# One PSUM tile for u and z of the 64-row jobs

**Chip, cores, metric.** One core of one Trainium2 chip. The metric is the time of one execution on the device in microseconds, lower is better; runs that are compared come from the same rounds on the same chip. In this program the engine PE does the matmuls, ACT and DVE work on their results, and SP issues the transfers of the output. PSUM holds the tiles that matmuls write, SBUF the others.

## The reference, cut to what matters

The program is forgetting attention followed by a spectral mix and a ReLU. Only its end matters here:

```python
u = x + y                                    # x: attention, y: filtered in 64 Fourier modes
return u + np.maximum(u @ w_ch, 0.0)         # 8 batches x 576 rows x 512, float32, 9.44 MB
```

With z = u @ w_ch, the kernel has x and x @ w_ch (`XW`) in SBUF already; in its last 32 us it adds the last modes of y to both, in PSUM, and writes u + max(z, 0).

## The kernel before

The 576 rows of a batch are four blocks of 128 and one of 64. The output stage runs 20 jobs: jobs 0-3, 5-8, 10-13 and 15-18 take two blocks, jobs 4, 9, 14 and 19 ("singles") the 64-row blocks of two batches. A PSUM tile `[128, 2, 512]` float32 is two banks of 512 columns; u has two tiles, z has two. A pair uses both banks of a tile, a single only the first.

```python
psPair = [{"u": psE, "z": psE}, {"u": psU}]          # later: psPair[1]["z"] = psX
def start(n, tags="uz"):
    return [psPair[n % 2][tag].tile([128, 2, D], F32, tag=tag, name="p" + tag) for tag in tags]
...
def emit_u(job, ps, u, split=False):                 # ACT takes u out of PSUM
    ...  nc.scalar.copy(u[:, bs, :], ps[0][:, bs, :])
def emit_o(job, ps, u, o, pair, split=False):        # DVE: max(z, 0) + u, then SP sends
    ...  nc.vector.scalar_tensor_tensor(o[:, bs, :], ps[1][:, bs, :], 0.0, u[:, bs, :], ALU.max, ALU.add)
    ...                                              # singles: 2 transfers from 64 partitions each
    ...                                              # pairs from job 7 on: rows of two jobs go together,
    ...                                              # 2 transfers of 512 KB from 128 partitions
for n, job in enumerate(jobs):                       # z of this job, u of the next one
    zs = terms(job, ps, 1, "xy" if n else "y")
    us = []
    if not last:
        nxt = start(n + 1)
        us = terms(jobs[n + 1], nxt, 0, "xy")
    ...
    elif wide(job):        run(zs); run(us)
    elif len(job) == 1:    run(us); run(zs)
    ...
    emit_u(jobs[n + 1], nxt, uo_n[0])
    emit_o(job, ps, *uo, n == 0)
```

(Cuts are marked by dots; two `run` calls are drawn on one line.) A tile is given to its next user when the last reader of the one before has finished with it.

The softmax here doesn't subtract the row's maximum and nothing guards it: scores larger than these inputs give would overflow.

## Time and profile before

| | before |
|---|---|
| median of the first 3 runs | 436.66 us (436.33 to 436.97) |
| PE, DVE, ACT busy | 368.1, 263.7, 224.4 us of 435.2 |
| bytes written | 9.44 MB, all in the last 32 us |
| DVE's last pass ends, SP's last issue ends | 427.1 us, 430.7 us |

Busy shares over the whole span say nothing about this change, because it lives in the last 7% of it. The view to read is the timeline of the output stage: who waits for whom around jobs 9, 14 and 19, and how full the DMA engines are meanwhile. The prediction shows those lines.

### The profile page before, as it was taken

How to read it: one execution, taken by the hardware profiler on the slowest of the kernel's cores; microseconds unless marked ns; L12 is line 12 of the kernel's file. 1: busy time of each engine (PE TensorE's matmuls, PEld its weight loads, DVE VectorE, ACT ScalarE, POOL GpSimd, SP SyncE). 2: the span in 40 equal slices, each digit the busy share in tenths (PEclk: the TensorE clock that was granted, in tenths of full speed). 3: DMA queues.
4: the chain of work that ended last, by engine and by line, in shares of the span. 5: the costliest groups of instructions: out<-in, count | busy, mean ns of one | idle time of the engine just before them, and what ended most of it. 6: DMA issues, size and time to landing. Idle time of an engine off the chain costs nothing.

```text
span 435.2 us, 12314 instructions
## 1 busy us (share of the span) xinstructions
PE 368.1 (85%) x5313; PEld 249.7 (57%) x5313; DVE 263.7 (61%) x659; ACT 224.4 (52%) x339; POOL 126.8 (29%) x198
## 2 busy tenths in 40 slices
PE   3787799999987879778787788799999998899881
PEld 2454566776666666566565666656665555454540
DVE  5797888876555655555557568533332665553892
ACT  2887488774526454365462646134434443631781
POOL 8333332333233233232333222223223223200400
PEclk9996899996558665586565869589999999989997
DMA  8999999999999999999999999999999999995797
GB/s 184 234 235 241 234 236 238 235 212 236 234 215 236 225 224 237 210 238 233 214 237 211 212 211 212 211 211 211 211 211 211 212 210 211 211 211 100 253 367 274
DMA packets 50982, 97.38 MB, mean 224 GB/s; under 512 B 3792, under 2 KB 12976, under 8 KB 50928
## 3 DMA queue, kind: packets, MB, share of 16 engines
q0 software_dynamic: 46560, 86.09, 100.9%
q1 hardware_dynamic: 4368, 10.51, 6.7%
q8 instruction: 41, 0.67, 0.6%
q14 instruction: 13, 0.11, 0.1%
HBM read 163.73 MB, written 9.44 MB: 398 GB/s over the span
## 4 chain that ended last, share of the span: by engine, by line
PE 35%; DMA 26%; ACT 12%; DVE 10%; issue 4%; SPq 0%; DVEq 0%; POOL 0%; ACTq 0%
DMA wb<-in_moe_w_i_dram 25%; ACT E L576 8%; PE pav L614 7%; PE ps L569 7%; PE A L188 6%; PE tp L307 5%; PE px L657 2%; PE vp L541 2%; DVE QTs L322 2%; ACT KT L320 2%; ACT VT L326 2%; DVE XT L671 1%; DVE os L1005 1%; DVE E L591 1%; PE px L682 1%
## 5 line engine op out<-in xcount | busy, mean ns | idle before, releaser
L576 ACT ACTIVATE E<-ps 128x1024 bf16<-128x1024 f32 (+1 forms) x128 | 101.5, 851 | 26.1 <-PE ps L569 15.4
L93 POOL DMA_DIRECT2D wb<-in_moe_w_r_dram x64 | 42.5, 664 | 128.9 <-PE A L188 25.1
L188 PE MATMUL A<-XT,wb 128*128 128x16 bf16 x1984 | 69.9, 181 | 8.2 <-DMA wb<-in_moe_w_i_dram 3.8
L188 PEld LDWEIGHTS <-wb 128*128 128x128 bf16 x1984 | 63.5, 100 | 22.8 <-issue 11.9
L569 PE MATMUL ps<-QTs,KT 64*128 64x64 bf16 (+4 forms) x384 | 60.2, 334 | 16.6 <-ACT E L576 14.7
L93 POOL DMA_DIRECT2D wb<-in_moe_w_i_dram x64 | 42.3, 661 | 77.5 <-DMA wb<-in_moe_w_i_dram 32.5
L614 PE MATMUL pav<-va,E 128*128 128x65 bf16 (+1 forms) x1088 | 57.1, 214 | 3.2 <-DVE x_all L636 2.6
L614 PEld LDWEIGHTS <-E 128*128 128x128 bf16 (+1 forms) x1088 | 47.0, 118 | 16.9 <-issue 7.0
L591 DVE TENSOR_TENSOR E<-E,trimask 128x256 bf16<-128x256 bf16 (+2 forms) x128 | 36.9, 303 | 20.0 <-ACT E L576 19.8
L326 ACT COPY VT<-tp 128x640 bf16<-128x640 bf16 (+1 forms) x32 | 23.2, 761 | 33.4 <-PE tp L307 33.4
L867 ACT CAST XW<-pxw 128x512 bf16<-128x512 f32 x36 | 20.7, 586 | 35.9 <-PE pxw L860 28.3
L569 PEld LDWEIGHTS <-KT 64*128 64x128 bf16 x384 | 19.4, 100 | 33.6 <-issue 22.8
L860 PE MATMUL pxw<-wch,yy 128*128 128x512 bf16 x144 | 36.0, 388 | 0.0
L320 ACT COPY KT<-tp 128x640 bf16<-128x640 bf16 (+1 forms) x32 | 21.9, 749 | 26.0 <-PE tp L307 25.8
L910 ACT CAST XW<-pB 128x512 bf16<-128x512 f32 x36 | 21.0, 585 | 25.4 <-PE pB L828 25.3
L909 DVE CAST x_all<-pA 128x512 bf16<-128x512 f32 x36 | 24.9, 692 | 14.2 <-PE pA L828 12.5
L322 DVE COPY QTs<-tp 128x640 bf16<-128x640 bf16 (+1 forms) x32 | 23.4, 767 | 14.3 <-PE tp L307 14.0
L636 DVE TENSOR_TENSOR x_all<-pav,rcp 128x384 bf16<-128x384 f32 x64 | 29.1, 455 | 0.9
L625 DVE RECIPROCAL rcp<-pav 128x6 f32<-128x6 f32 x64 | 12.1, 189 | 25.1 <-PE pav L614 24.3
L828 PEld LDWEIGHTS <-ident_bf 64*64 64x64 bf16 (+1 forms) x348 | 15.7, 108 | 17.9 <-issue 9.3
L153 DVE TENSOR_TENSOR YTe<-A,Yacc 128x128 bf16<-128x128 f32 x16 | 5.9, 367 | 33.3 <-PE A L188 33.3
L541 PE MATMUL vp<-ident_bf,VT 128*128 128x128 bf16 x160 | 18.4, 261 | 4.6 <-DVE QTs L322 3.9
(142 smaller groups left out, 617.4 us busy)
## 6 DMA issues: line engine op xcount, KB each, us to landing
wb<-in_moe_w_r_dram POOLq DMA_DIRECT2D x62, 512.0 KB, 16.7
wb<-in_moe_w_i_dram POOLq DMA_DIRECT2D x62, 512.0 KB, 17.3
stv<-in_v_dram POOLq DMA_DIRECT2D x10, 576.0 KB, 15.2
out_dram<-os SPq DMA_DIRECT2D x10, 512.0 KB, 4.5
stk<-in_k_dram POOLq DMA_DIRECT2D x11, 288.0 KB, 15.3
stq<-in_q_dram POOLq DMA_DIRECT2D x11, 288.0 KB, 15.1
wx<-in_v_dram POOLq DMA_DIRECT2D x5, 576.0 KB, 15.4
out_dram<-uo SPq DMA_DIRECT2D x3, 512.0 KB, 3.6
```

Source lines behind the costliest of these rows:

```text
L93: keep(nc.gpsimd.dma_start(dst, src))
L188: ins = nc.tensor.matmul(A[:, eb, mi, :], lhsT=w_of(mi, eb * 128), rhs=x_of(m), start=(i == 0), stop=(i == len(terms) - 1),)
L320: nc.scalar.copy(rows(KTs[pr % 2][:, :, 0:S]), tv)
L322: ins = nc.vector.tensor_copy(rows(QT[pr][:, :, :]), tv)
L326: nc.scalar.copy(rows(VTs[pr % 2][:, :, 0:S]), tv)
L541: nc.tensor.transpose(vp[:, sc, :, :].rearrange("p b d -> p (b d)"), VTs[s // 2 % 2][:, h, sc * 128 : (sc + 1) * 128], ident_bf[:, :],)
L569: nc.tensor.matmul(ps[:, b, o : o + n], lhsT=KTs[pr % 2][bs, h, jb * 128 : (jb + 1) * 128], rhs=QT[pr][bs, h, jb * 128 + c0 : jb * 128 + c ...
L576: nc.scalar.activation(E[:, :, piece * 512 : piece * 512 + w], ps[:, :, 0:w], ACT.Exp, scale=scale,)
L591: nc.vector.tensor_tensor(dg, dg, tr, ALU.mult)
L614: nc.tensor.matmul(pav[64 * half : 64 * half + w, slot, :], lhsT=E[:, b, c : c + (w - 1) * st + 1 : st], rhs=va[:, jb, b, :], start=(n == ...
L636: nc.vector.tensor_tensor(xo, pi, ri, ALU.mult)
L860: nc.tensor.matmul(pxw[:, :], lhsT=xT[:, eb, i * 128 : (i + 1) * 128], rhs=wch[:, eb, :], start=(eb == 0), stop=(eb == NDC - 1),)
```

## The change

Its intent: a single needs only one bank for u and one for z. If both lie in the single's u tile, the z tiles are left to the pairs, and z of the pair behind a single finds a tile that has been free for a while.

```diff
-        def start(n, tags="uz"):
-            return [
-                psPair[n % 2][tag].tile([128, 2, D], F32, tag=tag, name="p" + tag)
-                for tag in tags
-            ]
+        def bank(tag, n):
+            return psPair[n % 2][tag].tile([128, 2, D], F32, tag=tag, name="p" + tag)
+
+        def start(n):
+            u = bank("u", n)
+            if len(jobs[n]) == 1:
+                return [u[:, 0:1, :], u[:, 1:2, :]]
+            return [u, bank("z", sum(len(j) == 2 for j in jobs[:n]))]
```

## The prediction

> **What bounds the kernel now.** I read first the page, then the list of waits from 408 us on, then the timeline of the last 28 us engine by engine, and last the busy time and DMA rate in half-microsecond stretches. The change touches only the output stage, so what bounds the first 400 us (the weight transfers, 25% of the chain that ended last) is out of it.
>
> The output stage has 20 jobs. Jobs 0 to 3, 5 to 8, 10 to 13 and 15 to 18 are pairs of row blocks (PSUM tiles of two banks), jobs 4, 9, 14 and 19 are the 64-row singles. Each job is: PE writes u and z into PSUM, ACT copies u out (L1000), DVE forms max(z,0)+u from PSUM and the copy (L1005), SP sends the rows out. I told the jobs apart in the timeline by counting: the 692 ns forms of L1005 on 128x512 at 415.09, 420.76 and 426.46 are jobs 9, 14 and 19.
>
> The waits from 408 us on (waiting group, what ended it, us in total, times, longest):
> ```profile
> ACT us L1000 <- PE pu L828: 3.2, 5, 1.0
> PE pz L828 <- DVE os L1005: 1.8, 5, 0.5
> DVE os L1005 <- issue: 0.7, 2, 0.5
> PE pz L828 <- DVE uo L1005: 0.7, 1, 0.7
> ```
> PE waits 2.5 us in six places for DVE to free z's banks. Those behind singles are what the change aims at. Around job 9:
> ```profile
> 414.61 0.38 PE L828 MATMUL pz<-yy,BIl 64*64 64x512 bf16 x2
> 415.19 0.37 PE L828 MATMUL pz<-x_all,ident_bf 64*64 64x512 bf16 x1 [0.20 <-DVE os L1005]
> 415.62 0.38 PE L828 MATMUL pu<-x_all,ident_bf 64*64 64x512 bf16 x1
> 415.09 0.69 DVE L1005 SCALAR_TENSOR_TENSOR uo<-pz,uo 128x512 f32<-128x512 f32 x1
> 415.93 1.23 DVE L1005 SCALAR_TENSOR_TENSOR os<-pz,us 128x1024 f32<-128x1024 f32 x1
> 416.31 1.01 ACT L1000 COPY us<-pu 128x1024 f32<-128x1024 f32 x1 [0.69 <-PE pu L828]
> 417.36 1.23 DVE L1005 SCALAR_TENSOR_TENSOR os<-pz,us 128x1024 f32<-128x1024 f32 x1 [0.20 <-ACT us L1000]
> ```
> z of job 9 is through at 415.0. z of job 10 starts at 415.19, when job 8's DVE pass (413.92 + 1.23 = 415.15) has left the bank. u of job 11 follows on PE at 415.62, ACT copies it at 416.31, and only then (417.36) can DVE take job 11. So the DVE gap ahead of job 11 is set by u of job 11, not by z.
>
> But does DVE set the end? The stretches (length, busy time of PE, PEld, DVE, ACT, POOL, then granted clock, DMA share, GB/s):
> ```profile
> 416.00:418.00 2.00, 1.91 (x39) 1.07 (x29) 1.79 (x2) 1.69 (x2) 0.00 (x0) 1.00 1.02 395
> 418.50:419.00 0.50, 0.37 (x8) 0.25 (x9) 0.50 (x2) 0.50 (x1) 0.00 (x0) 1.00 0.92 279
> 419.00:419.50 0.50, 0.50 (x14) 0.30 (x8) 0.50 (x1) 0.33 (x1) 0.00 (x0) 1.00 0.54 143
> 419.50:420.00 0.50, 0.50 (x12) 0.43 (x8) 0.50 (x2) 0.27 (x1) 0.00 (x0) 1.00 0.98 209
> 420.50:424.00 3.50, 2.98 (x48) 1.64 (x48) 3.11 (x4) 2.66 (x3) 0.00 (x0) 1.00 1.03 411
> 426.00:431.00 5.00, 0.08 (x2) 0.00 (x0) 1.14 (x2) 0.02 (x1) 0.00 (x0) 0.78 1.02 408
> ```
> DVE is done at 427.1 while the DMA engines carry 408 GB/s until 431. SP shows why:
> ```profile
> 416.08 2.60 SPq L1012 DMA_DIRECT2D out_dram<-uo  x2
> 418.76 3.30 SPq L1025 DMA_DIRECT2D out_dram<-os  x4
> 422.16 2.69 SPq L1012 DMA_DIRECT2D out_dram<-uo  x2
> 424.94 3.22 SPq L1025 DMA_DIRECT2D out_dram<-os  x4
> 428.25 2.49 SPq L1012 DMA_DIRECT2D out_dram<-uo  x2
> ```
> From 418.76 SP issues without a break worth naming; job 19's rows, ready at 427.1, are issued at 428.25. From there the end is a sum of bytes: four pairs of 2 x 512 KB and two singles of 2 x 128 KB are 4.72 MB; at 408 GB/s that is 11.6 us, and with about 1 us from issue to full rate it gives 431.4, as seen. The last moment at which the DMA engines ran dry is 418.5 to 420.0 (about 0.7 us lost, worked out from 279, 143 and 209 against 408 GB/s). So the end hangs on when rows 10 and 11 go out: job 11's DVE pass ends at 417.36 + 1.23 = 418.59, while SP is free of job 9's issues at 416.08 + 2.60 = 418.68.
>
> **What the Trainium skill says.** "PSUM — Partial Sum Buffer", section "Engine vs sequencer instructions": matmuls start and complete in program order. The trace agrees: u of job 11 (415.62) stands behind z of job 10 (415.19), so a wait moved from z to the u behind it still stops PE. "Perfetto Trace Analysis", section "Matmuls": independent groups should rotate through banks so that emptying one overlaps filling the next; the trace shows the lack of it as the 0.2 to 0.7 us waits of pz, which is the change's intent. The same page, section "What 'DMA-bound' means": a solid row of DMA instructions on the issuer points to the issuer as the bound, that window being descriptor generation. Here SP is solid, yet the engines carry 408 GB/s at share 1.02, so I take the solid row as back-pressure, not as the bound. "DMA: Bandwidth & Descriptors", section "Where 436 GB/s comes from", gives 435 GB/s for the ports and about 358 for one core's HBM share; the trace's 408 lies above the second, so near the first there is little left.
>
> **The change, part by part.** No instruction is added or removed: the same matmuls, copies, DVE passes and transfers. Only tiles move.
>
> Part 1, z of a pair. It alternated by job number, so z of job n waited for DVE of job n-2. Now it alternates by the count of pairs. After a single, z of job n waits for n-3: z of 5 for job 2 (not 3), z of 10 for 7 (not 8), z of 15 for 12 (not 13). One job later, 6, 11 and 16 wait for the pair ahead and no longer for the single. Worth: z of job 10 starts right behind z of job 9, about 414.6 to 414.8 instead of 415.19; DVE's job 10 can follow job 9's pass at about 415.75 instead of 415.93 (passes follow a 692 ns one after 0.6 us): 0.18 us earlier. z of job 5, waiting now until 409.39, starts near 408.5; DVE's job 5 moves from 410.48 to about 409.9, 0.6 us earlier.
>
> Part 2, the single's u tile. It now holds z as well, so it is freed by the single's DVE pass and no longer by ACT's short copy. The next user is u two jobs on: u of 6 waits for DVE's job 4, u of 11 for job 9, u of 16 for job 14. Job 9's pass ends at 415.09 + 0.69 = 415.78. With job 8's pass perhaps 0.07 later, u of job 11 can start at about 415.89, against 415.62 now: 0.27 us later. ACT's copy goes from 416.31 to 416.58, DVE's job 11 from 417.36 to 417.63, its end from 418.59 to 418.86. What part 1 gave job 10 is not passed on, as job 11 was held by u and is held longer. For job 6 the same: job 4's pass ends at 409.94, u of 6 goes from 409.82 to 409.98, DVE's job 6 from 411.62 to about 411.72, so the 0.6 us of job 5 shrink to -0.1 within one job. For job 16: job 14's pass ends near 421.44 + 0.27, u moves from 421.32 to about 421.75, DVE's job 16 from 423.06 to about 423.5.
>
> Part 3, the path that sets the end. SP sends rows 10 and 11 after job 11: now 418.76, then about 418.86 + 0.09 = 418.95, so 0.19 us later, with the engines dry meanwhile. Everything behind follows at the DMA rate. Job 16 would end at 424.7 against an issue at 424.94 (+0.19), job 19 at 427.6 against 428.25: both hidden. Earlier gains (jobs 5 and 10) land ahead of the dry spell and vanish in it. Sum: +0.19 us, 436.66 + 0.19 = 436.85.
>
> **The rivals.** One: u does not wait for the single's pass as I read it (because the release is kept by bank, say), and the intent holds. Then z of 10 and u of 11 move up by about 0.4 us, DVE's job 11 starts at 416.9, and rows 10 and 11 are ready at 418.1. SP still has to finish job 9's issues at 418.68, itself held by back-pressure, so the direct gain is under 0.1 us; with some of the dry spell filled it could reach 0.7 us at most: 436.0 to 436.6. For it speaks that the DMA has a hole of just that size; against it SP's 416.08 + 2.60. Two: DVE is the bound, at 1.79 of 2.00 us busy from 416 to 418. Then the moved wait on u costs 0.27 to 0.43 us per single, and three singles give up to 1.0 us: 437.6. Against it: job 19's rows wait 1.1 us for SP, so the tail hides most. Three: the end is bytes alone and all shifts are hidden: 436.66. Four: the order of instructions on PE comes out different because the tiles differ; that could go either way by some tenths.
>
> **Range and chances.** The whole stage lasts 32 us, its floor is 9.44 MB written at 408 GB/s, 23 us; no step above is worth over 1 us, and 2% would be 8.7 us. Three runs of the kernel before spread 0.64 us. So the range is rival one's floor to rival two's ceiling, nearly: 436.1 to 437.5. Faster or slower by 2% would need something unseen; 0.01 each.
>
> **What would show it.** Right: L1005 of job 10 moves up beside job 9; pu of job 11 waits for DVE uo where it waited for none; ACT's copy ahead of job 11 starts near 416.6; the DMA hole at 419 is as deep or longer; SP's issue of rows 10 and 11 near 418.95. Wrong: pu of job 11 starts near 415.2 and DVE's job 11 before 417.3, or the hole at 419 fills. The prediction fails altogether if the instructions of the first 400 us are placed differently, which nothing in the change asks for.

## The result, and the profile after

The changed kernel took 437.13 us (median of 6, 436.39 to 438.34), the kernel before 436.82 us (median of 6, 436.33 to 437.03). The ratio is 1.0013, with a 95% interval of 0.9997 to 1.0029. A ratio is the mean time of one kernel's fast runs over that of the other's of the same rounds, so not quite the ratio of the medians quoted.

The profiled run after happened to be a short one (434.7 us against 435.2), so spans do not tell the two apart. Positions inside the stage do. I count them from the first DVE pass of job 0 (403.99 before, 403.85 after), and write +13.37 for 13.37 us after it. PE's order of matmuls is the same in both kernels until the output stage (the first that differs is number 5,102 of 5,313, at +4.1), and there it differs only around the singles.

Who waited for whom from 404 us on, after:

```profile
DVE os L1008 <- ACT us L1003: 1.9, 3, 0.6
PE pz L828 <- DVE os L1008: 1.9, 3, 0.6
PE pu L828 <- DVE uo L1008: 1.5, 3, 0.7
PE pu L828 <- ACT uo L1003: 1.2, 3, 0.7
```

The two last rows are new. The first of these is the wait that the prediction moved from z to u; the second, PE held by ACT's copy of a single's u, it did not name. "PE pz <- DVE uo", 0.7 us before, has gone: the intent is met. Around job 9, PE, then DVE, then ACT:

```profile
414.58 0.40 PE L828 MATMUL pu<-XW,ident_bf 64*64 64x512 bf16 x2 [0.25 <-ACT uo L1003]
415.01 0.37 PE L828 MATMUL pz<-x_all,ident_bf 64*64 64x512 bf16 x1
416.04 0.37 PE L828 MATMUL pu<-x_all,ident_bf 64*64 64x512 bf16 x1 [0.41 <-DVE uo L1008]
415.29 0.69 DVE L1008 SCALAR_TENSOR_TENSOR uo<-pu,uo 128x512 f32<-128x512 f32 x1 [0.24 <-issue]
415.90 1.21 DVE L1008 SCALAR_TENSOR_TENSOR os<-pz,us 128x1024 f32<-128x1024 f32 x1
417.75 3.49 DVE L1008 SCALAR_TENSOR_TENSOR os<-pz,us 128x1024 f32<-128x1024 f32 x3 [0.64 <-ACT us L1003]
416.71 2.84 ACT L1003 COPY us<-pu 128x1024 f32<-128x1024 f32 x3 [1.27 <-PE pu L828]
```

The matmuls at 414.58 are z of job 9; they carry the name pu because they write the u tile now. They wait 0.25 us for ACT's copy of u out of the other bank. DVE's job 9 (415.29) therefore has a gap of 0.24 us ahead of it. z of job 10 starts at once (414.6 to 415.01). u of job 11 (416.04) waits for DVE's job 9 to end, ACT's copy follows, and DVE's job 11 (417.75, at +13.90 against +13.37) has a gap of 0.64 us where it had 0.20. SP after:

```profile
416.01 2.10 SPq L1015 DMA_DIRECT2D out_dram<-uo  x2
419.00 3.09 SPq L1028 DMA_DIRECT2D out_dram<-os  x4
422.20 2.31 SPq L1015 DMA_DIRECT2D out_dram<-uo  x2
425.19 3.17 SPq L1028 DMA_DIRECT2D out_dram<-os  x4
428.46 2.47 SPq L1015 DMA_DIRECT2D out_dram<-uo  x2
```

SP is no longer solid: it is free at 418.11 and issues rows 10 and 11 at 419.00, free at 424.51 and issues rows 15 and 16 at 425.19. It now waits for DVE. But its issues take less time each, and the DMA rate is what it was:

```profile
418.50:420.00 1.50, 0.97 (x18) 0.72 (x20) 1.50 (x2) 1.05 (x2) 0.00 (x0) 1.00 0.70 213
426.00:431.00 5.00, 0.89 (x8) 0.14 (x3) 2.12 (x3) 0.58 (x1) 0.00 (x0) 1.00 1.00 399
```

(Same columns as in the prediction; the DMA share is the mean busy share of the 16 DMA engines.) I call the stretch of low rate behind a single a hole. The hole behind job 9 moves 213 GB/s against 210 in the same 1.5 us before (the mean of the prediction's three stretches), and the tail 399 against 408. DVE ends 1.4 us later, SP's last issue begins 0.27 us later (+25.75 against +25.48), and the data cease (the last packet of output begins) at +28.6 after and +29.0 before, where the last 0.7 us is a trickle under 125 GB/s. These ends scatter by some tenths from profile to profile, so a shift of 0.2 us is not to be seen in them.

### The profile page after: what moved, and what is told of

The parts are those of the page before. It is cut to its first block, busy times and chain, and to the rows that moved or that the text cites. A ratio compares the mean times of both kernels' runs of the same rounds, so it can differ in the third digit from the quotient of the medians.

```text
span 434.7 us, 12314 instructions
## 1 busy us (share of the span) xinstructions
PE 363.7 (84%) x5313; PEld 246.8 (57%) x5313; DVE 263.0 (61%) x659; ACT 223.6 (51%) x339; POOL 126.9 (29%) x198
## 4 chain that ended last, share of the span: by engine, by line
DMA 43%; PE 23%; ACT 10%; DVE 7%; issue 4%; POOL 1%; ACTq 0%
DMA wb<-in_moe_w_i_dram 39%; ACT E L576 6%; PE pav L614 5%; PE ps L569 5%; PE A L188 4%; PE tp L307 4%; DMA stv<-in_v_dram 3%; DVE QTs L322 2%; ACT KT L320 2%; ACT VT L326 1%; PE vp L541 1%; PE px L657 1%; PE px L682 1%; POOL yy L823 1%; PE pu L828 1%
## 5 line engine op out<-in xcount | busy, mean ns | idle before, releaser
L569 PE MATMUL ps<-QTs,KT 64*128 64x64 bf16 (+4 forms) x384 | 57.6, 320 | 18.1 <-ACT E L576 16.3
L614 PE MATMUL pav<-va,E 128*128 128x65 bf16 (+1 forms) x1088 | 55.6, 210 | 3.1 <-DVE x_all L636 2.6
L614 PEld LDWEIGHTS <-E 128*128 128x128 bf16 (+1 forms) x1088 | 45.6, 115 | 17.4 <-issue 8.0
L910 ACT CAST XW<-pB 128x512 bf16<-128x512 f32 x36 | 20.8, 586 | 29.7 <-PE pB L828 29.6
L636 DVE TENSOR_TENSOR x_all<-pav,rcp 128x384 bf16<-128x384 f32 x64 | 29.1, 455 | 0.9
L541 PE MATMUL vp<-ident_bf,VT 128*128 128x128 bf16 x160 | 17.2, 249 | 4.7 <-DVE QTs L322 4.2
```

The source lines that it names most:

```text
L569: nc.tensor.matmul(ps[:, b, o : o + n], lhsT=KTs[pr % 2][bs, h, jb * 128 : (jb + 1) * 128], rhs=QT[pr][bs, h, jb * 128 + c0 : jb * 128 + c ...
L614: nc.tensor.matmul(pav[64 * half : 64 * half + w, slot, :], lhsT=E[:, b, c : c + (w - 1) * st + 1 : st], rhs=va[:, jb, b, :], start=(n == ...
L636: nc.vector.tensor_tensor(xo, pi, ri, ALU.mult)
```

## The experiments

**The changed kernel again.**

> The changed kernel unaltered, beside the kernel before on one chip, to size the scatter. Times below are counted from the first DVE pass of job 0. In the first profiles DVE's job 11 started at 13.37 us before and 13.90 after, SP sent rows 10 and 11 at 14.77 before and 15.15 after, and the last issue came at 24.26 before and 24.61 after; yet the profiled run after was the shorter one. Theory (two new waits in each single, mostly hidden under the transfers): the positions repeat to 0.1 us, the time is 0 to 0.15% above before. Rival (the +0.13% is scatter alone and nothing in the stage moved it): the ratio changes sign or the positions do not repeat.

Measured: 436.74 us against 437.01 before, ratio 1.0000 (0.9985 to 1.0015). The positions repeat to 0.03 us: DVE's job 11 at +13.91, job 19 at +23.83, SP's last issue at +25.74. (The "last issue" of the expectation, 24.26 and 24.61, is the first of job 19's two.) So the shifts within the stage are real and exact, and the time does not resolve them. Most of the scatter comes from ahead of the stage: over the 14 kernels profiled, with the same work up to there, the first DVE pass of job 0 lies anywhere from 403.44 to 405.45 us.

**Sharing without the counting by pairs.**

```diff
-            return [u, bank("z", sum(len(j) == 2 for j in jobs[:n]))]
+            return [u, bank("z", n)]
```

> The single still shares its tile, but z of pairs alternates by job number as in the kernel before: part 2 without part 1. Theory (the harm comes from sharing alone): DVE's job 11 starts at 13.8 to 14.1 after the first pass, as in the changed kernel (13.90), PE's u of job 11 still waits for DVE's job 9, z of the singles still waits for ACT's copy; time within 0.1% of the changed kernel. Rival (the counting by pairs moved things): job 11 starts near 13.4, as before.

Measured: 436.87 us, ratio to the kernel before 1.0000 (0.9984 to 1.0016). DVE's job 11 is at +13.91, as in the changed kernel; both new waits are there. Among the passes only job 5 differs: +6.49 as before, where the changed kernel has +5.87. So the counting by pairs gives its 0.6 us to job 5 and nothing to job 11 or later; the harm comes from the sharing alone.

**u dodges the single's tile.** The job two behind a single takes the other u tile, which job n-1 has and which ACT frees. The diff leaves out four lines that build the list `UI`.

```diff
-            u = bank("u", n)
+            u = bank("u", UI[n])     # UI alternates, but stays put two jobs behind a single
```

> The changed kernel, but u of the second job after a single goes to the other u tile, which is freed by ACT's copy of the job between (in the changed kernel that copy of job 10 ends 0.54 us before DVE's job 9). Theory (the single's tile, held until DVE's pass, is what delays u of job 11): u of job 11 starts about 0.5 us earlier than in the changed kernel, DVE's job 11 starts at 13.3 to 13.5 in place of 13.90, the DVE gap of 0.64 us ahead of it shrinks to about 0.1; time 0.1 to 0.4 us under the changed kernel's, about as before. Rival (ACT's copies or SP set the pace, not u's bank): job 11 stays at 13.8 or later.

Measured: 436.31 us against 437.01, ratio 0.9994 (0.9978 to 1.0010).

```profile
416.68 0.37 PE L828 MATMUL pu<-x_all,ident_bf 64*64 64x512 bf16 x1
417.09 4.80 DVE L1008 SCALAR_TENSOR_TENSOR os<-pz,us 128x1024 f32<-128x1024 f32 x4
```

Its first pass is at 405.45, so u of job 11 starts at +11.23 (+12.19 in the changed kernel), with no wait noted, and DVE runs four pairs from job 10 on without a gap: job 11 at +12.95, ahead of the kernel before (+13.37). The tile held until DVE's pass is what delayed u. The gain at job 11, 0.96 us, is more than the 0.5 expected, because the same cure at job 6 (+7.30 against +7.73) is carried along. SP sends rows 10 and 11 at +14.25 and begins its last issue at +24.81; the data cease at +28.0.

**z of the single right behind its u.**

```diff
-            zs = terms(job, ps, 1, "xy" if n else "y")
+            zs = terms(job, ps, 1, "xy" if n else "y") if len(job) == 2 else []
...
                 us = terms(jobs[n + 1], nxt, 0, "xy")
+                if len(jobs[n + 1]) == 1:
+                    us = us + terms(jobs[n + 1], nxt, 1, "xy")
```

> The changed kernel, but the single's z matmuls are placed right behind its u matmuls, one job earlier in the order, ahead of ACT's copy. Theory (z of a single waits for ACT's copy of u in the same tile, 0.25 us for jobs 9 and 14, 0.68 us for job 19; the prediction had not named this wait): the wait of pu-tile matmuls on ACT's uo copy vanishes, DVE's job 9 follows job 8 without the 0.24 us gap, DVE's job 11 starts at 13.6 to 13.7 in place of 13.90, and job 19 starts 0.5 us or more earlier than 23.82; ACT's copy of u may now wait for z instead, which costs it 0.2 us of idle time that it has. Time 0 to 0.3 us under the changed kernel's. Rival (the wait named is not what holds DVE): job 9 keeps its gap.

Measured: 437.11 us, ratio 1.0009 (0.9994 to 1.0024). The wait on ACT's copy has gone, and DVE's job 9 follows job 8 without a gap:

```profile
414.94 0.68 DVE L1008 SCALAR_TENSOR_TENSOR uo<-pu,uo 128x512 f32<-128x512 f32 x1
417.39 3.49 DVE L1008 SCALAR_TENSOR_TENSOR os<-pz,us 128x1024 f32<-128x1024 f32 x3 [0.64 <-ACT us L1003]
```

Job 11 is at +13.57, at the edge of what was expected, job 19 at +22.83: taking the unnamed wait away gains 0.34 us at job 11 and 1.0 at job 19. The other gap of 0.64 us stays, as u of job 11 still waits for the single. The time did not fall; SP's last issue stayed at +25.87.

**Both remedies.** The edits of the last two together.

> Both remedies in the changed kernel: u of the second job after a single goes to the other u tile, and z of the single stands right behind its u. Times from the first DVE pass of job 0. Theory (the two waits are separate and add): u_dodge took 0.96 us off the start of DVE's job 11 (13.91 to 12.95) and 1.50 off job 19 (23.82 to 22.32); z_first took 0.34 off job 11 and 1.0 off job 19; together job 11 starts near 12.6 and job 19 near 21.3, no DVE gap over 0.25 us behind a single. The last issue of SP then comes 0.5 to 1.3 us before that of the kernel before (24.26), as far as the transfers let it; time 0.5 to 1.2 us under the kernel before. Rival (transfers set the end whatever DVE does): the last issue stays within 0.3 us of u_dodge's 23.61 and the time with it.

Measured: 435.58 us against 436.88, ratio 0.9977 (0.9958 to 0.9995). They do not add: job 11 at +13.06 and job 19 at +22.14, not 12.6 and 21.3. With z directly behind u, ACT's copy of job 9 comes 0.1 us later (+9.79 against +9.68 in u_dodge), with it the copy of job 10, whose end (+11.29) is what u of job 11 (+11.34) waits for. So the chain ACT copy, u, ACT copy sets job 11 there. The rival's "within 0.3 us of u_dodge" holds for SP too: the first of its last two issues is at 23.82 against 23.61.

**Once more.**

> The version with both remedies once more, on another day of the chip, since the first time its lead was 0.23% with an interval that ends at 0.9995. Theory (its engines are done about 0.3 us before those of the kernel before, and its last issue comes 0.5 us earlier): 0.05 to 0.25% faster than the kernel before, positions of DVE's passes within 0.05 us of the first run (job 11 at 13.06, job 19 at 22.14). Rival (the lead was scatter): ratio 0.9995 to 1.001.

(The "other day" of the expectation was nine minutes later on another chip.) Measured: 436.44 us against 436.32, ratio 0.9995 (0.9981 to 1.0008). The positions repeat (job 11 at +13.06, job 19 at +22.14, last issue at +25.02 against +25.48 before), the lead in time does not: by the time measured it is the rival's result. A stage shorter by some tenths is in all three profiles of the versions that dodge (data cease at +28.0, +28.1 and +28.3, against +28.6 to +29.1 in the kernels before and after, in sharing alone and in z_first); that it makes the kernel faster is not shown beyond the scatter.

**Where these tenths are won or lost** can be read off the kept traces. The rate from +26.0 to +29.5, times 3.5 us, is the output still to be moved at +26.0. Before, after, sharing alone, u_dodge:

```profile
429.99:433.49 3.50, 0.00 (x0) 0.00 (x0) 0.00 (x0) 0.00 (x0) 0.00 (x0) 0.50 0.68 236
429.85:433.35 3.50, 0.00 (x0) 0.00 (x0) 0.00 (x0) 0.00 (x0) 0.00 (x0) 0.68 0.71 246
430.60:434.10 3.50, 0.00 (x0) 0.00 (x0) 0.00 (x0) 0.00 (x0) 0.00 (x0) 0.50 0.82 281
431.45:434.95 3.50, 0.00 (x0) 0.00 (x0) 0.00 (x0) 0.00 (x0) 0.00 (x0) 0.50 0.48 159
```

That is 826, 861, 984 and 557 KB. At +17.0, just past the hole behind job 9, the same count gives 4,350, 4,325, 4,513 and 4,113 KB. So the lead of u_dodge and the lag of sharing alone are there already at +17; all that the engines do later shifts them by 70 KB at most, under 0.2 us. The other profiles fit: z_first, with job 19 a microsecond earlier than in the changed kernel, has as much left as sharing alone (4,525 and 984 KB); both remedies have 4,150 and 4,200, then 592 and 641 KB. The order at +17 follows, but for a tie of before and after, the moment when SP's first issue of rows 10 and 11 ends: +14.90, +14.97 and +15.13 in the versions that dodge, +15.31 before, +15.50 after, +15.99 and +16.00 in sharing alone and z_first. This is an agreement of kept traces, not a test of its own. Its start does not tell: in z_first it begins at +14.83, before that of the changed kernel, but takes 1.18 us in place of 0.34. What makes it so long no run shows.

**Less output, before and after.** The pairs from job 7 on send half of their rows, a wrong result.

```diff
-                    rs = slice(sb % 2 if n_wide < 2 else 0, sb % 2 + 1)
+                    rs = slice(sb % 2, sb % 2 + 1)
```

> The kernel before with the wide pairs sending only one of their two rows per partition: half of their output is not written, so the result is wrong on purpose. It takes load off the DMA engines and leaves the work of PE, ACT and DVE alone. Theory (the transfers hide what DVE does late): with them out of the way SP's last pair of issues follows DVE's job 19 at once, at 23.2 to 23.3 after the first pass, and the time falls by 2 to 3.5 us against the kernel before. Rival (engines set the end already): the time falls by under 1 us.

> The changed kernel with the same halved output, wrong on purpose as well. Theory (the change makes the engines' part 1.35 us longer at job 19, 23.82 against 22.47, and the transfers hide most of it): the last issues come at 24.5 to 24.7, and the time is 1.0 to 1.5 us above that of the kernel before with halved output, where the whole kernels differ by 0.1% or less. Rival (the change costs the engines nothing that counts): the two halved kernels are within 0.4 us.

Measured: 434.27 us for before halved, 435.00 for after halved; ratios to the whole kernel before 0.9940 (0.9920 to 0.9959) and 0.9960 (0.9940 to 0.9980). The last two issues of SP, before halved, then after halved (first passes at 403.60 and 404.42):

```profile
427.08 1.12 SPq L1012 DMA_DIRECT2D out_dram<-uo  x2
```

```profile
428.96 1.12 SPq L1015 DMA_DIRECT2D out_dram<-uo  x2
```

That is +23.48 and +24.54: 1.06 us apart, where the whole kernels are 0.27 to 0.35 apart. Halving took 2.6 us off the kernel before, so the transfers do set its end. With the load off, the change costs something in time as well: 0.7 us by the medians, and 0.0020 of 436.9, or 0.9 us, by the ratios. That is at or under the least of the 1.0 to 1.5 expected, because in the kernel before SP was still busy with job 18's rows when job 19 was done (+23.14), and used up 0.3 us of the 1.35. The two intervals overlap, but both hold the scatter of the same whole kernel. Compared directly, six runs each, the means are 434.08 and 435.07: 0.99 us apart, with a 95% interval of about 0.2 to 1.8 worked out from these runs. The 1.06 us between the issues agree with it.

**The singles' transfers on POOL.** What makes the holes in the DMA rate, DVE or something else? (The edit is to the kernel before.)

```diff
-                        nc.sync.dma_start(
+                        pool_dma(
                             out[b + h, 512:576, :], o[64 * h : 64 * h + 64, 0, :]
                         )
```

> The kernel before with the transfers of the singles (128 KB each) issued by POOL in place of SP. In the profile before, each dip of the DMA rate (143 to 279 GB/s near 419, 254 to 258 near 425.5) comes right after SP had spent 2.6 us in issuing a single's two transfers, with the next pair's rows ready within 0.1 us of it or well before. Theory (the prediction's step that the dry spell at 419 is set by when rows 10 and 11 are ready is incomplete: SP is held by the single's small transfers, which keep the engines fed for only 0.3 us each): the dips shrink by half or more, rows 10 and 11 are issued at about 14.7 as DVE allows, rows 15 and 16 (ready at 20.3) are issued at 20.4 and not at 20.95, the time falls by 0.2 to 0.8 us. Rival (the dips are DVE's doing alone): the dip at 419 is as before and the time is within 0.2 us.

Measured: 438.04 us against 436.88, ratio 1.0036 (1.0013 to 1.0059): slower. The issues moved as expected (rows 10 and 11 at +14.63, rows 15 and 16 at +20.33), the hole near +15 was less deep (246 GB/s at the least, against 131), but the 3 us from +25.5 ran at 246 to 352 GB/s. Yet the data ceased at +29.0, as in the kernel before: a large part of the loss is not in the flow of data. A run's time is 2.2 us longer than its span here, 2.0 us in before_pool3 below and 1.7 us in every other kernel, so about 0.5 of the 1.2 us lies outside the span. A version with only job 19 back on SP (`if b == B - 2`) followed.

> The kernel before with the transfers of jobs 4, 9 and 14 issued by POOL and those of job 19 by SP again. With all four on POOL the kernel was 0.36% slower although rows 10 and 11 went out at 14.63 and rows 15 and 16 at 20.33, and its last 5 us moved only 230 GB/s. Theory (POOL's last transfers, beside SP's last pair, made the slow end): with job 19 on SP the end is as before and the earlier issues remain, 0 to 0.3% faster than the kernel before. Rival (any single sent beside SP's pairs costs more than it frees): slower again by 0.1 to 0.4%.

Measured: 436.53 us against 436.32, ratio 0.9999 (0.9986 to 1.0012). The loss has gone, and no gain is left in the time, although rows 15 and 16 went out at +20.34 in place of +20.95. (0.3 us of its time lie outside the span; the spans average 434.5 us against 434.8 before. The expectation's 230 GB/s is of a stretch that ends 0.8 us after the data ceased.) The holes remain near +15 and +21 (221 and 197 GB/s at the least). Why transfers by POOL lengthen what lies outside the span stays open.

**What flows slowly: short runs, or few partitions?** Two edits of the kernel before, on four pairs alone. I had miscounted when I wrote what was expected: the condition picks jobs 7, 8, 10 and 11, not 10 to 13; the bytes, 2.1 MB, are the same. One sends each job's rows by itself (2 KB runs, 128 partitions):

```diff
-                elif sb % 2 or n_wide < 2:
-                    rs = slice(sb % 2 if n_wide < 2 else 0, sb % 2 + 1)
+                elif sb % 2 or n_wide < 6:
+                    rs = slice(sb % 2 if n_wide < 6 else 0, sb % 2 + 1)
```

> The kernel before, with the rows of jobs 10, 11, 12 and 13 sent each job by itself (transfers of 256 KB from 128 partitions, 2 KB in one run) in place of two jobs together (512 KB, 4 KB in one run). Job 10's rows are then ready at 13.2 after the first pass and no longer wait for job 11. Theory A (the prediction's: the dip at 419 is a dry spell, and ends when rows 10 and 11 are ready): job 10's rows go out as soon as SP is free, the dip shrinks, 0 to 0.3 us faster. Theory B (the dips of 210 to 256 GB/s at a DMA share of 0.8 to 0.9 are the singles' own 262 KB in transfers of 2 KB runs, which flow slowly): the rate falls below 300 GB/s wherever the 2 KB runs flow, 2.1 MB of them, and the time rises by 1.5 to 3.5 us. Theory C (the dips are the singles', but because only 64 partitions are read): no fall of the rate and no gain, within 0.3 us.

The other cuts each transfer by partitions (4 KB runs, 64 partitions):

```diff
+                        for p0, pn in ((0, 64), (64, 64)) if 2 <= n_wide < 6 else ((0, 128),):
                             nc.sync.dma_start(
-                                out[...][:, rs, :], pair[:, j, rs, :],
+                                out[...][p0 : p0 + pn, rs, :], pair[p0 : p0 + pn, j, rs, :],
                             )
```

> The kernel before, with each transfer of jobs 10 to 13 cut into two by partitions (64 partitions each, 256 KB, still 4 KB in one run). Theory C (transfers from 64 partitions flow slowly, near 250 GB/s, as the singles' do at 425 to 426): the rate over these 2.1 MB falls below 320 GB/s and the time rises by 1 to 3 us. Theory A or B: the rate stays near 400 and the time within 0.4 us of the kernel before.

Measured: by itself, 437.02 us, ratio 1.0005 (0.9990 to 1.0020); cut by partitions, 439.37 us, ratio 1.0060 (1.0047 to 1.0073), against 436.32. DMA share and GB/s (the last two columns), by itself, then cut by partitions:

```profile
418.50:421.50 3.00, 2.33 (x36) 1.22 (x29) 3.00 (x3) 2.52 (x4) 0.00 (x0) 1.00 0.81 239
421.50:426.00 4.50, 3.88 (x60) 2.03 (x60) 4.11 (x5) 3.44 (x4) 0.00 (x0) 1.00 1.01 387
```

```profile
415.50:418.00 2.50, 2.20 (x40) 1.08 (x32) 2.29 (x2) 2.08 (x3) 0.00 (x0) 1.00 0.83 205
418.00:418.75 0.75, 0.59 (x10) 0.36 (x11) 0.75 (x2) 0.75 (x1) 0.00 (x0) 1.00 0.05 16
418.75:424.00 5.25, 4.33 (x71) 2.50 (x68) 4.86 (x6) 3.99 (x6) 0.00 (x0) 1.00 0.90 265
424.00:426.00 2.00, 1.53 (x16) 0.39 (x9) 2.00 (x3) 1.15 (x2) 0.00 (x0) 1.00 0.89 270
```

The second group covers the rows of jobs 7, 8, 10 and 11 and the single between them: from 64 partitions at a time they flow at 205 to 270 GB/s with a DMA share of 0.83 to 0.90, apart from a dry 0.75 us (16 GB/s) that begins while SP ends an issue of 2.28 us. It costs 2.6 us, the dry stretch included. In the first pair the upper line holds the end of jobs 7 and 8, a dry half microsecond (78 GB/s) and job 9's two transfers, the lower one the rows of jobs 10 and 11 in 2 KB runs, and of 12 and 13, at 387 GB/s. Both edits double the number of transfers, so that is not what slows the flow. Theory C holds and B falls. A is not tested by this: SP took longer over the smaller transfers (5.36 us for eight from 412.66, against 4.16 for six before), sent job 10's rows only at +15.54, and began its last issue at +26.69; the data ceased at +29.7, later than before, though the time hardly shows it.

This is what the Trainium skill says in "SBUF — State Buffer", section "Door 1: The DMA port swizzle (why `[64,N]` ≈ `[32,N]`)": 64 partitions reach 8 of 16 ports, with about 218 GB/s as their limit. The trace is near it at first, 205 GB/s, and over it later, 265 and 270. The section "Can I just issue two DMAs to hit both halves?" measured only 6% more from two transfers, one in each half, than from one; before_part64, with both halves queued in turn, agrees in part: its 270 GB/s stay far from the 387 of whole transfers, but they are a quarter over that limit, and from 421.52 to 422.02, when most packets were of job 9's two transfers, the rate was 377.

The holes are thus, for the greater part, the singles' own transfers: each single sends 262 KB from 64 partitions at a time. The packets kept in the trace bear this out. From 418.5 to 420.0 in the kernel before, 118 packets of 2 KB began, which only the single sends then, and 18 of 4 KB. Those of 2 KB took 136 ns on the mean, against 86 ns for the 2 KB packets of jobs 10 and 11 in before_split6 (422 to 424); the 4 KB packets took 215 to 257 ns in the stretches of before_part64, against 163 in the kernel before (420.5 to 424). But a single is not slow everywhere: in before_part64 job 9's packets took 88 ns. Whether two halves in flight at once make the difference no run shows, and a single sent from all 128 partitions was not tried.

## Why the prediction was right or wrong

The time was right: 436.85 us predicted in 436.1 to 437.5, measured 437.13 and 436.74. The ratio is within 0.15% of 1, and the predicted +0.19 us cannot be told from nothing. That says little for the working: the range also held rival three's 436.66 and most of rival one's, and two of its errors offset each other, which is luck. Step by step:

- **Part 1, z of the next pair.** Right for job 5 (0.6 us predicted, 0.62 measured: 6.49 to 5.87), which shrank to +0.08 at job 6 (+0.1 predicted). Wrong for job 10, "0.18 us earlier": it came 0.11 us later (11.94 to 12.05), because job 9 itself was late.
- **Part 2, the single's u tile.** The mechanism was right: u of 11 waits for DVE's job 9, and u_dodge takes this away. The size, "0.27 us later" at DVE's job 11, was half of the 0.53 measured. The term missing from the sum is z of the single waiting for ACT's copy of u out of the same tile, although it writes the other bank: it made DVE's job 9 0.35 us late, where the prediction allowed 0.07, and without it (z_first) job 11 came 0.34 us earlier. I had read the tile's next user and overlooked its second user.
- **Part 3, "Job 16 ... job 19 ...: both hidden".** Failed for job 16: it ended at +21.32, and SP, free since +20.66, sent rows 15 and 16 at +21.34. Job 19 ended at +24.51, just when SP got free. The waits of three singles piled up to 1.35 us, not to rival two's 1.0 us.
- **"The last moment at which the DMA engines ran dry is 418.5 to 420.0."** Failed for the most part. The DMA share in that hole, 0.92, 0.54 and 0.98, stood in my own quotation: engines mostly busy, at half their rate. before_part64 shows that transfers from 64 partitions run so. Only the middle half microsecond has a share that speaks of idle engines. So most of the hole could not be filled by rows 10 and 11. It can grow, though: in sharing alone and in z_first 0.75 us at 63 and 33 GB/s follow it, with shares of 0.18 and 0.10.
- **"The end hangs on when rows 10 and 11 go out."** Borne out between versions, not for this change. The lead or lag that a version has at the end is there once the hole behind job 9 is past, and goes with the end of the first issue of rows 10 and 11. But in the changed kernel that issue began 0.38 us later (+15.15 against +14.77) and ended only 0.19 us later, as it took 0.34 us in place of 0.54. At +17 no lag is to be seen, and at +26 there are 35 to 42 KB more to move, 0.1 us at 408 GB/s (an estimate). before_pool3 sent rows 15 and 16 out 0.6 us earlier and gained nothing in time, but it is no clean test, as part of its time lies outside the span. For the change itself, rival three (bytes alone) comes nearest.
- **"It gives 431.4, as seen."** Not as seen: the view it was held against ends at 431, and the data ceased at 433.0. The sum took 408 GB/s for the singles too. Their 0.52 MB at 210 to 256 GB/s, as in the holes, take 0.8 to 1.2 us more (an estimate); the slow trickle at the end makes up most of the rest.

Two errors, then, in opposite directions: the engines' delay was under-sized by a factor of two, and its way to the end was over-stated. The halved kernels show how much the transfers hide: with the load off, 1.06 us of the delay reach SP's last issues, and with the load on about 0.3. What stays open is what makes SP's issues long or short, and where the 2 us of scatter ahead of the stage come from; it hides anything under 0.1% here.

## What to carry to other kernels

Sharing a tile removes one wait and lengthens the tile's life to that of its slowest reader: list every later user of the tile, and every pair of accesses within it, before counting a gain. Before calling a stretch of low DMA rate a dry spell, look at the share beside it: here a share near 1 at half the rate was a slow shape of transfer, and only what was dry behind it could be won by an earlier issue. When a time does not resolve a change, positions counted from a fixed event of the stage do, to 0.03 us here.

## What the Trainium skill lacked or had wrong

- "Perfetto Trace Analysis", section "What 'DMA-bound' means", names engines, issuer and SBUF reads; it has no word on transfers from half of the partitions, which here kept SP solid and the engines at a share of 0.83 to 0.90 at 205 to 270 GB/s. The "SBUF — State Buffer" page has the cause, but its table stops short of saying how it looks in a profile.
- "DMA: Bandwidth & Descriptors", section "Where 436 GB/s comes from", says that about 358 GB/s binds between HBM and SBUF; the output here ran at 408 GB/s over 5 us (426 to 431, kernel before), with one core running. The passage does not say that a core alone can get more, though the page says so elsewhere.
- No page that I read says that matmuls into one bank of a PSUM tile may be held for a copy out of its other bank (by the framework's bookkeeping of whole tiles, I suppose; no run tests that): 0.25 us for jobs 9 and 14 and 0.68 us for job 19 in the changed kernel, gone in z_first. "PSUM — Partial Sum Buffer", section "PSUM bank collisions raise a hardware error", asks for waits by bank and quadrant of partitions, or simply by bank.
